# Attention laid out in a new order: score groups cut anew, every PSUM bank counted, small results in `av`'s spare columns

## The chip, the core and the metric

The kernel runs on one NeuronCore of a Trainium2 chip, as one program. The metric is the device time of one launch in microseconds. The profile is one execution of that program as the hardware profiler recorded it; times in it count from its first instruction.

## What is computed

Three layers follow one another: an attention with a memory term, a mixture of experts whose tokens are assigned greedily, and a dense layer with a maximum of three products. The change touches the first alone.

```python
def _attn_ref(q, k, v, M_prev, z_prev, beta):      # B, H, S, D = 4, 8, 576, 64
    scores = scale * np.matmul(q, k.transpose(0, 1, 3, 2))
    scores = np.where(causal, -1000000000.0, scores)
    scores = scores - scores.max(-1, keepdims=True)
    a = np.exp(scores)
    a /= a.sum(-1, keepdims=True) + 1e-09
    local = np.matmul(a, v)
    ...
    mem_out = mem_ret / mem_norm                   # phi(q) @ M_prev, phi(q) @ z_prev
    g = 1.0 / (1.0 + np.exp(-beta))[None, :, None, None]
    return (g * mem_out + (1 - g) * local).astype(np.float32)

x = attn_out.transpose(0, 2, 1, 3).reshape(B * S, H * D)
x = _moe_ref(x, ...)      # 8 experts of 288 tokens each, chosen by descending logit
return _moe2_ref(x, ...)  # max(x @ w1, x @ w2, x @ w3) @ w_out
```

## The kernel before

Attention works on 16 pairs of heads. The two heads of a pair lie on partitions 0 to 63 and 64 to 127, so that two products with 64 rows each, one for each head, run beside one another on TensorE. The 576 queries and keys are five tiles `j` and `kb` of 128 (the last one 64).

For one pair the work is as follows.

- SP loads `KR`, `QN`, `MZ`, `V` and `VT`. ScalarE casts keys and queries to `KH` and `QH` (fp32r), VectorE takes the rests `KL` and `QL`.
- A first, coarse pass of scores finds each query's maximum. It comes in pieces (`piece`, L409): query tile 3 (keys up to 512), tile 2 (384), tiles 1 and 0 (256 and 128), and tile 4 through the spread operand `qj` (L406). Every piece writes two buffers of the ring `st`, five PSUM banks in all. VectorE masks and reduces them into `nm` (L418, L422), ten reductions a pair.
- The nine columns of maxima are cast (L451, `nmr`), transposed on TensorE (L455, which writes one more buffer of `st`), copied out (L459, `nmt`) and sent by three DMAs (L464, L466) into a row tile, also called `nm`, that the exact scores subtract.
- The exact scores come transposed (keys on partitions) in three groups (`score`, L582), each of which writes two buffers of `st`, one for each head. A key tile's columns are four products for each head: `KH` by `QH`, `KL` by `QH`, `KH` by `QL`, and the subtraction of `nm`. Group 0 is key tile 0 with queries 0 to 512; group 1 is key tile 0 with the last 64 queries and key tile 1 with its 448; group 2 is key tile 2 with 320 and key tile 3 with 192, and then key tile 4 (64 by 64) in two further buffers. ScalarE takes exp of each buffer into `pt` (L608, L606), GpSimd masks the diagonal (L629). With each group goes one piece of the coarse pass of the pair two further on.
- `av` (L622) multiplies `pt` by `V`: ten products for each head with 128 columns of weights and five with 64 (query tile 4). It gathers in `AV`, a tile of two banks, one for each head, of which 365 of 512 columns are used. VectorE normalises it (L655 to L670).
- Beside this: `mem` (L529, five products of `phi` and `MZ` in two parts), and a gate product (L481, five of `VT` and `wb`, whose last has 64 columns of weights), all into the bank `MEM`. The dense layer's weights are converted meanwhile (`conv`, L825 to L866).

Ahead of the first exact scores TensorE runs 78 small products on zeros (L746, `warm`), spread between what it waits for.

The order of all this is made when the program is built. Each piece of work is a task with a key (10 for each pair, plus a number of the table `PRIO`), a cost for each engine that may run it, its predecessors, and the buffers that it takes. `Plan.run` schedules them greedily: of the tasks that could start earliest by the costs and by a table of latencies it takes the one with the smallest key. A task that takes a buffer of a full ring waits for the users of the oldest one. The engines then run their instructions strictly in the order so found. In `Plan.run` the count for a task that takes several buffers of one ring reads

```python
for b in t.new:
    k = len(b.ring.made) - b.ring.n
    if k >= 0:
        users += b.ring.made[k].users
```

and `made` grows only when the task is placed, so that each of the task's buffers looks at the same, oldest one.

## Time and profile before

| | us |
|---|---|
| time, median of 3 runs | 861.74 (859.13 to 865.17) |
| time of the profiled execution | 861.3 |
| its span, first to last instruction | 859.6 |
| TensorE busy in the span | 818.2 (95%) |
| VectorE busy | 552.6 (64%) |
| ScalarE busy | 341.5 (40%) |
| TensorE's granted clock, 0 to 20 us and 20 to 40 us | 1.00 and 0.66 |
| first exact scores start | 25.36 |
| second pair's exact scores start | 41.31 |
| last pair's exact scores start | 257.60 |

Attention takes the first 271 us; from there to about 300 us the first expert's tokens are chosen, mostly on VectorE, and the rest is the experts and the dense layer. `PE` is TensorE's matmuls, `PEld` its weight loads, `SPq` the DMA issues on SyncE's queue. A "busy" TensorE is one with a matmul in flight.

### The profile page before, as it was taken

To read this page: it belongs to the slowest core of one execution; us is meant where nothing else is said; L and a number is where in the kernel's file an instruction comes from. 1 tells how busy PE (TensorE), PEld (TensorE's weight loads), DVE (VectorE), ACT (ScalarE), POOL (GpSimd) and SP (SyncE) were. 2 spreads that over 40 slices of the span, in tenths; PEclk is the share of its full clock that TensorE was granted. 3 is DMA by queue.
4 is the path that set the end of the run, shared out by engine and by line. 5 is a ranking of instruction groups with operands and counts; after the bars stand their busy time and mean duration, and the time that the engine had idled before them with its cause. 6 is when DMAs were issued, how large, how long until landed. Compare 5 with 4: busy or idle time off the path is not lost.

```text
span 859.6 us, 17881 instructions
## 1 busy us (share of the span) xinstructions
PE 818.2 (95%) x6906; PEld 756.0 (88%) x6906; DVE 552.6 (64%) x1610; ACT 341.5 (40%) x871; POOL 102.2 (12%) x241
## 2 busy tenths in 40 slices
PE   8899999999996599999999999999999999999996
PEld 6788888888785499999999999999999999999996
DVE  7578889878834787886864874873774643532321
ACT  2567666566545432234214214313412422522311
POOL 2212112113212100101010010002002011000001
PEclk9699999999998599999999999999999999999999
DMA  5544655645402541425104404402412541450000
GB/s 157 164 142 142 194 159 176 192 145 168 148 5 70 134 105 37 135 91 175 50 29 146 76 18 127 106 1 94 121 48 60 165 42 36 151 46 26 26 1 38
DMA packets 39606, 84.80 MB, mean 99 GB/s; under 512 B 11552, under 2 KB 14304, under 8 KB 39520
## 3 DMA queue, kind: packets, MB, share of 16 engines
q1 hardware_dynamic: 35648, 72.87, 30.1%
q0 software_dynamic: 3872, 10.78, 4.3%
q8 instruction: 54, 0.88, 0.5%
q14 instruction: 32, 0.26, 0.1%
HBM read 72.77 MB, written 9.74 MB: 96 GB/s over the span
## 4 chain that ended last, share of the span: by engine, by line
PE 74%; issue 16%; DVE 5%; ACT 3%; POOL 1%; DMA 0%; DVEq 0%; POOLq 0%; ACTq 0%
PE av L622 12%; PE w L1300 10%; PE w L1302 10%; PE w L1301 10%; PE st L582 6%; PE acc L1300 5%; PE acc L1301 5%; PE acc L1302 5%; PE mem L529 3%; PE mem L481 2%; PE rps L1042 2%; ACT x L552 1%; PE st L409 1%; PE av L746 1%; DVE junk L422 1%
## 5 line engine op out<-in xcount | busy, mean ns | idle before, releaser
L1300 PE MATMUL w<-yh,mh 128*128 128x288 f32 x576 | 174.1, 302 | 0.0
L1302 PE MATMUL w<-yh,ml 128*128 128x288 f32 x576 | 169.8, 295 | 0.0
L1301 PE MATMUL w<-yl,mh 128*128 128x288 f32 x576 | 169.5, 294 | 0.0
L622 PE MATMUL av<-V,pt 128*128 128x112 f32 (+1 forms) x960 | 112.5, 266 | 0.3 <-DVE r L689 0.3
L1300 PEld LDWEIGHTS w<-yh,mh 128*128 128x128 f32 x576 | 108.6, 189 | 2.7
L1301 PEld LDWEIGHTS w<-yl,mh 128*128 128x128 f32 x576 | 108.3, 188 | 2.9
L622 PEld LDWEIGHTS av<-V,pt 128*128 128x128 f32 (+1 forms) x960 | 98.6, 173 | 13.7 <-issue 8.9
L1302 PEld LDWEIGHTS w<-yh,ml 128*128 128x128 f32 x576 | 108.3, 188 | 0.0
L1270 DVE TENSOR_TENSOR wlo<-wraw,whi 128x1024 fp32r<-128x1024 f32 x64 | 78.2, 1222 | 36.0 <-ACT whi L1266 35.8
L1407 DVE TENSOR_TENSOR mt<-w,mt 128x288 f32<-128x288 f32 x96 | 43.6, 454 | 80.2 <-PE w L1302 79.3
L422 DVE CUSTOM_DVE_ANT_0 junk<-st,mask 128x384 bf16<-128x384 f32 (+3 forms) x144 | 66.2, 460 | 27.2 <-PE st L409 14.7
L1266 ACT CAST whi<-wraw 128x1024 fp32r<-128x1024 f32 x64 | 66.8, 1049 | 30.7 <-PE acc L1301 21.5
L1301 PE MATMUL acc<-hl,whi 128*128 128x288 f32 x256 | 76.0, 297 | 1.4 <-DVE hl L1218 0.9
L1300 PE MATMUL w<-xhi,whi 128*128 128x288 f32 x256 | 76.5, 299 | 0.0
L1302 PE MATMUL w<-xhi,wlo 128*128 128x288 f32 x256 | 76.3, 298 | 0.2 <-DVE wlo L1270 0.2
L1300 PE MATMUL acc<-hh,whi 128*128 128x288 f32 x256 | 76.3, 298 | 0.0
L1301 PE MATMUL w<-xlo,whi 128*128 128x288 f32 x256 | 76.2, 298 | 0.0
L1302 PE MATMUL acc<-hh,wlo 128*128 128x288 f32 x256 | 75.3, 294 | 0.0
L1162 ACT CAST gc<-mt 128x32 fp32r<-128x32 f32 (+2 forms) x72 | 17.5, 243 | 140.8 <-DVE mt L1407 140.8
L608 ACT ACTIVATE pt<-st 128x512 f32<-128x512 f32 x96 | 52.8, 610 | 39.3 <-PE st L582 39.3
L1218 DVE SCALAR_TENSOR_TENSOR hl<-w,hh 128x288 fp32r<-128x288 f32 x64 | 29.2, 456 | 60.7 <-ACT hh L1212 60.6
L1243 POOL DMA_INDIRECT xg<-xd,tidx x24 | 24.1, 1002 | 351.2 <-PE w L1302 240.1
(236 smaller groups left out, 1727.3 us busy)
## 6 DMA issues: line engine op xcount, KB each, us to landing
wraw<-in_wr SPq DMA_DIRECT2D x64, 512.0 KB
m2raw<-in_m2w SPq DMA_DIRECT2D x12, 512.0 KB
V<-in_v SPq DMA_DIRECT2D x16, 365.0 KB
KR<-in_kN SPq DMA_DIRECT2D x16, 288.0 KB
QN<-in_qN SPq DMA_DIRECT2D x16, 288.0 KB
VT<-in_vT SPq DMA_DIRECT2D x16, 288.0 KB
xd<-x SPq DMA_DIRECT2D x16, 256.0 KB
m2raw<-in_m2w SPq DMA_DIRECT2D x12, 256.0 KB
```

Source lines behind the costliest of these rows:

```text
L422: V.tensor_tensor_reduce(out=junk[:, :w], in0=o.s[x][:, c:c + w], in1=m, scale=1.0, scalar=-3.0e38, op0=OP.add, op1=OP.max, accum_out=r.nm ...
L529: PE.matmul(MEM[:m, 2 * C * jj:2 * C * jj + 2 * C], r.phi[:, 128 * j:128 * j + m], r.MZ, start=True, stop=True)
L582: PE.matmul(d[:kr, c:c + z - a], neg[q, :kr] if wt is None else wt[q, k], mv[q, a:z], start=x == 0, stop=x == 3)
L608: A.activation(r.PT[:, i, 512 * gi:512 * gi + 512], o.t[i], AF.Exp, scale=0.125)
L622: PE.matmul(AV[:m, i, j * C:j * C + w], r.PT[:, i, o:o + m], r.V[:, c:c + w], start=kb == 0, stop=kb == j)
L1218: V.scalar_tensor_tensor(lo(), src(), 0.0, hi().bitcast(F32), op0=OP.max, op1=OP.subtract)
L1266: A.copy(x.W[fb][0], x.RAW[fb])
L1270: V.tensor_sub(x.W[fb][1], x.RAW[fb], x.W[fb][0].bitcast(F32))
L1300: nc.tensor.matmul(o, wh, rh, start=start, stop=False)
L1301: nc.tensor.matmul(o, wh, rl, start=False, stop=False)
L1302: nc.tensor.matmul(o, wl, rh, start=False, stop=stop)
L1407: V.tensor_max(q.mt, o.pt[:, :T], q.mt)
```

## The change

- The score groups are cut anew: group 0 is key tile 0 with queries 0 to 256 and key tile 1 with 128 to 384; group 1 key tile 0 with 256 to 576 and key tile 3; group 2 key tile 2 with 256 to 576 and key tile 1 with 384 to 576 (and, as before, key tile 4). The layout of `pt` follows (`COLS`).
- `Plan.run` counts each buffer that a task takes of a ring for itself. It also knows a price for a change between products with 64 and with 128 rows (`SWITCH`), and keeps TensorE off a bank of `AV` whose readers are not done (`held`).
- Of the coarse pass of query tile 4 the last 64 columns, and the transposed maxima, no longer take buffers of `st`: they go into columns 384 to 512 of `AV`.
- The last products of `mem` and of the gate get all 128 columns of weights: `phi` and `VT` become fixed tiles of 640 columns with zeros at the end.
- The first pairs' `KR` and `QN` are loaded first; the first pair's maxima become urgent work (`CRIT`); costs of DMA issues and all of `PRIO` have new numbers.

After attention the instructions of every engine stand in the same order as before.

```diff
+COLS = {(0, 0): 0, (0, 1): 128, (0, 2): 512, (0, 3): 640, (0, 4): 768, (1, 1): 256, (1, 2): 384, (1, 3): 1344, (1, 4): 1472,
+        (2, 2): 1024, (2, 3): 1152, (2, 4): 1280, (3, 3): 832, (3, 4): 960, (4, 4): 1536}
...
-        "T": (-1.2, 4.7, 5.8), "qj": "POOL", "nslack": 600, "A": (4.1, 6.4, 7.6, 8.7, 8.8), "norm": 15.3, "gate": 6, "m2": (4, 6.0, 10),
+        "phi": -3.6, "mem": (-0.3, 4.8), "memx": "ACT", "T": (-0.8, 4.2, 1.2), "qj": "POOL", "nslack": 600,
+        "A": (3.8, 6.6, 6.1, 9.4, 11.9), "norm": 13.6, "gate": 6, "m2": (4, 6.0, 7.8), "tmg": (1.1, 4.1, 12.7, 10.2), "lag": 6}
...
+WAIT, LD = 200, 700
+SWITCH = 135
...
-                blocked, users = False, []
+                users, taken = [], {}
                 for b in t.new:
-                    k = len(b.ring.made) - b.ring.n
-                    if k >= 0:
+                    k = len(b.ring.made) + taken.get(b.ring, 0) - b.ring.n
+                    taken[b.ring] = taken.get(b.ring, 0) + 1
+                    if 0 <= k < len(b.ring.made):
                         users += b.ring.made[k].users
+                users += held.get(t.bank, [])
...
-                    if e == "PE" and now < self.cold:
-                        c *= 2
+                    if e == "PE":
+                        c = c * (1 + (now < self.cold)) + SWITCH * (t.mode != mode)
...
+PHI = cs.tile([128, 640], F32, name="phi")
+    VT = [cs.tile([128, 640], F32, name=f"vt{k}") for k in range(BUFS["VT"])]
...
+        k1 = (-27, -26, -13.85)[p] if p < 3 else k0
...
-        tK = load("KR", [128, S], kN[b, pp], k0 - 3 * (p == 0), 1200)
+        tK = load("KR", [128, S], kN[b, pp], k1, LD)
...
-            o.bs, o.deps, o.key = [Buf(R["st"]) for _ in range(2)], [tqh, tkh, tj], key
+            tail = cuts[0][0] == 4
+            o.bs, o.deps, o.key = [Buf(R["st"]), Buf(R["aq" if tail else "st"])], [tqh, tkh, tj], key
...
+                    o.s = [ps.tile([128, 512], F32, name="st", bufs=BUFS["st"]) for _ in o.bs[tail:]] + [AV[:, 1, 384:]] * tail
...
-        kn = n + W["N"]
-        bn = Buf(R["st"])
+        kn = n + W["N"] if p else CRIT - 10
+        bn = Buf(R["an"])
...
-            r.pn = ps.tile([128, 512], F32, name="st", bufs=BUFS["st"])
-            PE.matmul(r.pn[:9, :128], r.nmr, identr, start=True, stop=True)
+            PE.matmul(AV[:9, 0, 384:], r.nmr, identr, start=True, stop=True)
...
-                PE.matmul(MEM[:rows(j), 4 * C + 16 * j:4 * C + 16 * j + w], r.VT[:, 128 * j:128 * j + rows(j)],
+                PE.matmul(MEM[:, 4 * C + 16 * j:4 * C + 16 * j + w], r.VT[:, 128 * j:128 * j + 128],
...
-                    m = rows(j)
-                    PE.matmul(MEM[:m, 2 * C * jj:2 * C * jj + 2 * C], r.phi[:, 128 * j:128 * j + m], r.MZ, start=True, stop=True)
+                    PE.matmul(MEM[:, 2 * C * jj:2 * C * jj + 2 * C], r.phi[:, 128 * j:128 * j + 128], r.MZ, start=True, stop=True)
...
-        groups = [[(0, 0, 512)], [(0, 512, 576), (1, 128, 576)], [(2, 256, 576), (3, 384, 576)]]
+        groups = [[(0, 0, 256), (1, 128, 384)], [(0, 256, 576), (3, 384, 576)], [(2, 256, 576), (1, 384, 576)]]
```

The first place is TensorE in the middle of a pair, from the end of one score group to the start of the next (`QL,KH` and `nm,neg` are the third and fourth products of a group; L409, and L429 after, is the coarse pass). Before, groups 1 and 2 stand back to back:

```order
L582 MATMUL st<-QL,KH 128x448 x2
L582 MATMUL st<-nm_129,neg 128x448 x2
L409 MATMUL st<-KH,QH 128x384 x2
L582 MATMUL st<-QH,KH 128x320 x2
L582 MATMUL st<-QH,KL 128x320 x2
```

and after, where group 2 comes first:

```order
L606 MATMUL st<-QL,KH 64x64 x2
L606 MATMUL st<-nm_129,neg 64x64 x2
L429 MATMUL st<-KH,QH 128x256 x2
L429 MATMUL st<-KH,QH 128x128 x2
L647 MATMUL av<-V,pt_131 64x73 x10
L506 MATMUL mem<-wb,vt_138 128x112 x4
L506 MATMUL mem<-wb,vt_138 128x16
L606 MATMUL st<-QH,KH 128x320 x2
```

The ten `av` products of query tile 4 and the gate's five moved between the two groups; the group that follows is the last of the pair.

The second place is TensorE where the first pair's exact scores begin. Before, both of the first products for the gate's constants (`wb,m2raw`), the second pair's transposed maxima and the first part of `mem` stand ahead of them:

```order
L746 MATMUL av<-warm 128x256
L765 MATMUL mem<-wb,m2raw 64x8 x8
L455 MATMUL st<-identr,nmr 9x128
L765 MATMUL mem<-wb,m2raw 64x8 x8
L529 MATMUL mem<-MZ,phi 128x146 x3
L582 MATMUL st<-QH,KH 128x512 x2
```

After, one set of `wb,m2raw` and then group 0 (eight rows, of which the last two stand here) come first:

```order
L606 MATMUL st<-QL,KH 128x256 x2
L606 MATMUL st<-nm_128,neg 128x256 x2
L429 MATMUL st<-KH,QH 128x512 x2
L553 MATMUL mem<-MZ,phi 128x146 x3
L479 MATMUL av<-identr,nmr 9x128
L426 MATMUL st<-KH,qj_126 128x512
L426 MATMUL av<-KH,qj_126 128x64
```

`mem`, the second set of `wb,m2raw` and the second pair's maxima moved behind the first score group, and the maxima and the last 64 coarse columns now write `av`.

The third place is SP's queue at the start, before:

```order
L349 DMA KR<-in_kN 128x576
L349 DMA QN<-in_qN 128x576
L349 DMA MZ<-in_mz 128x146
L349 DMA VT<-in_vT 128x576
L349 DMA V<-in_v 128x730
L275 DMA wb<-in_wg 64x4x8 x6
```

and after:

```order
L363 DMA KR<-in_kN 128x576
L363 DMA QN<-in_qN 128x576
L363 DMA KR<-in_kN 128x576
L363 DMA QN<-in_qN 128x576
L363 DMA MZ<-in_mz 128x146
L363 DMA V<-in_v 128x730
L373 DMA vt_137<-in_vT 128x576
L283 DMA wb<-in_wg 64x4x8 x6
```

The second pair's `KR` and `QN`, which stood behind the six `wb` transfers, now stand ahead of them; the third pair's follow right behind `wb`, and the first pair's maxima (`nm`) come before the second pair's `MZ`, `V` and `VT`.

## Rows read from the trace of the kernel before

**Rows 1.** Busy time by stretch: us, then busy us and instructions of each engine, PEclk, DMA

```profile
56.99:242.01 185.02, 176.71 (x1668) 152.29 (x1668) 154.45 (x484) 118.06 (x335) 39.10 (x129) 1.00 0.53 161
25.36:41.31 15.95, 15.21 (x113) 12.91 (x112) 8.30 (x30) 9.31 (x26) 3.59 (x10) 0.64 0.38 125
```

**Rows 2.** Waits, whole span: engine, what waited, releaser: us, times, longest

```profile
PE st L582 <- ACT pt L608: 7.4, 12, 1.1
```

**Rows 3.** Timeline of TensorE, one pair: start, us, line, out<-in, shape [idle before]

```profile
61.90 0.30 PE L582 MATMUL st<-QH,KH 64*128 64x64 f32 x2
...
63.25 0.34 PE L409 MATMUL st<-KH,QH 64*128 64x384 f32 x2
63.43 0.30 PE L582 MATMUL st<-QH,KH 64*128 64x320 f32 x1
64.64 0.41 PE L582 MATMUL st<-QH,KH 64*128 64x320 f32 x1 [0.91 <-ACT pt L608]
...
65.19 0.24 PE L582 MATMUL st<-QH,KH 64*128 64x192 f32 x1
```

**Rows 4.** Timeline of TensorE, group 2 of a late pair

```profile
248.34 0.31 PE L582 MATMUL st<-QH,KH 64*128 64x320 f32 x2
...
248.93 0.25 PE L582 MATMUL st<-QH,KH 64*128 64x192 f32 x2
...
249.36 0.20 PE L582 MATMUL st<-QH,KH 64*64 64x64 f32 x2
```

**Rows 5.** Timeline of TensorE from `av` into group 0

```profile
54.58 2.48 PE L622 MATMUL av<-V,pt 128*128 128x112 f32 x20
56.99 0.50 PE L582 MATMUL st<-QH,KH 64*128 64x512 f32 x2
...
58.03 0.39 PE L409 MATMUL st<-KH,QH 64*128 64x512 f32 x2
```

**Rows 6.** The same stretch asked from 56.72 on, so four of the twenty

```profile
56.45 0.61 PE L622 MATMUL av<-V,pt 128*128 128x112 f32 x4
```

**Rows 7.** Timeline of all engines at the start

```profile
6.14 0.75 DVE L501 SCALAR_TENSOR_TENSOR phi<-QN,ph 128x576 f32<-128x576 f32 x1
...
7.41 0.69 DVE L422 CUSTOM_DVE_ANT_0 junk<-st,mask 128x512 bf16<-128x512 f32 x1 [0.52 <-PE st L409]
...
10.36 1.26 PE L481 MATMUL mem<-wb,VT 128*128 128x112 f32 x10
...
11.56 2.36 PE L746 MATMUL av<-warm 128*128 128x256 bf16 x20
...
12.70 0.21 DVE L422 CUSTOM_DVE_ANT_0 junk<-st,mask 128x64 bf16<-128x64 f32 x1
...
16.95 0.30 PE L455 MATMUL st<-identr,nmr 128*9 128x128 f32 x1
...
18.29 1.24 SPq L466 DMA_DIRECT2D nm<-nmt  x2
...
19.44 0.64 PE L765 MATMUL mem<-wb,m2raw 128*64 128x8 f32 x16
...
22.59 0.67 ACT L295 CAST KH<-KR 128x576 fp32r<-128x576 f32 x1 [1.59 <-DMA KR<-in_kN]
...
23.63 1.80 PE L529 MATMUL mem<-MZ,phi 128*128 128x146 f32 x6 [2.24 <-issue]
...
25.36 0.79 PE L582 MATMUL st<-QH,KH 64*128 64x512 f32 x2
```

**Rows 8.** Waits of VectorE between 56.99 and 242.01 us, the two longest

```profile
DVE junk L422 <- PE st L409: 7.5, 18, 0.9
DVE rm L533 <- PE mem L529: 7.1, 14, 1.2
```

**Rows 9.** Timeline of a pair: coarse pass of query tile 4, and its second reduction

```profile
68.07 0.51 PE L406 MATMUL st<-KH,qj 128*128 128x512 f32 x2
...
70.84 0.21 DVE L422 CUSTOM_DVE_ANT_0 junk<-st,mask 128x64 bf16<-128x64 f32 x1
```

More of the change, by code (lines that the diff above doesn't have):

```diff
@@ L115, in __init__ @@
         self.new, self.use, self.end, self.lat, self.slack = [], [], None, None, 0
-        self.left, self.nexts = 0, []
+        self.left, self.nexts, self.mode, self.bank, self.readers = 0, [], 0, None, []
 class Plan:
@@ L148, in run @@
     def run(self):
-        free, order, now = {}, [], 0
+        free, order, now, mode, held = {}, [], 0, 0, {}
         for t in self.tasks:
@@ L198, in run @@
             t.end, t.eng = end, e
+            if e == "PE":
+                mode = t.mode
+                if t.readers:
+                    held[t.bank] = held.get(t.bank, []) + t.readers
             now = max(now, best[0])
@@ L275, in ldw @@
                 nc.sync.dma_start(WB[64 * i:64 * i + 64, a, :, i], wg.rearrange("(c i d) e -> i d c e", i=2, d=64)[i])
-    twb = add(-14.8, {"SP": 1200}, ldw)
+    twb = add(-13.9, {"SP": 4000}, ldw)
     cdone = constants(g, tc, consts, beta, add)
     R = {n: Ring(k) for n, k in BUFS.items()}
-    R["av"], R["mem"], R["xl"] = Ring(1), Ring(1), Ring(1)
+    for x in ("av", "mem", "an", "aq", "xl"):
+        R[x] = Ring(1)
     def tile(name, shape, dt=F32):
@@ L401, in fS @@
                 if not hasattr(o, "s"):
-                    o.s = [ps.tile([128, 512], F32, name="st", bufs=BUFS["st"]) for _ in o.bs]
+                    o.s = [ps.tile([128, 512], F32, name="st", bufs=BUFS["st"]) for _ in o.bs[tail:]] + [AV[:, 1, 384:]] * tail
                 for j, c in cuts:
@@ L430, in alone @@
         def alone(o):
-            o.after(add(o.key, {"PE": o.cost + 130}, o.fn, o.deps, new=o.bs + o.first, use=o.use))
+            t = add(o.key, {"PE": o.cost}, o.fn, o.deps, new=o.bs + o.first, use=o.use)
+            t.mode = 64 * (o is not r.last)
+            k = len(tred)
+            o.after(t)
+            if o is r.last:
+                t.bank, t.readers = 1, tred[k + 1:]
         ks = n + W["S"]
@@ L436, in pair @@
                               [(i, c, w, 4 * i + j) for i in range(2) for j, c, w in ((1, 0, 256), (0, 256, 128))]))
+        r.last = piece(ks + W["last"], [(4, 0)], [(0, 0, 512, 8), (1, 0, 64, 9)])
         if p < AHEAD:
@@ L439, in pair @@
                 alone(o)
-        r.last = piece(ks + W["ds"] * 3, [(4, 0)], [(0, 0, 512, 8), (1, 0, 64, 9)])
         alone(r.last)
         yield r
-        kn = n + W["N"]
-        bn = Buf(R["st"])
+        kn = n + W["N"] if p else CRIT - 10
+        bn = Buf(R["an"])
         def fx(e):
@@ L469, in pair @@
         t = add(kn, {"ACT": 100}, fn0, [t], new=[bf["nmr"]], use=[bf["nm"]])
-        t.slack = W["nslack"]
-        t = add(kn, {"PE": 110}, fn1, [t], new=[bn], use=[bf["nmr"]])
-        t = add(kn, {"ACT": 140}, fn2, [t], new=[bf["nmt"]], use=[bn])
-        r.tN = add(kn + .1, {"SP": 1500}, fn3, [t, tnm[p] if p < len(NM) else None], new=[bf["NM"]], use=[bf["nmt"]], lat=NLAT)
+        t.slack = W["nslack"] if p else 0
+        tt = add(kn, {"PE": 110}, fn1, [t], new=[bn], use=[bf["nmr"]])
+        t = add(kn, {"ACT": 140}, fn2, [tt], new=[bf["nmt"]], use=[bn])
+        tt.bank, tt.readers = 0, [t]
+        r.tN = add(kn + .1, {"SP": 1900}, fn3, [t, tnm[p] if p < len(NM) else None], new=[bf["NM"]], use=[bf["nmt"]], lat=NLAT)
         bG = Buf(R["mem"])
@@ L492, in phi1 @@
         def phi1(e):
-            r.phi = tile("phi", [128, S])
+            r.phi = PHI
             r.ph = tile("ph", [128, S])
@@ L596, in score @@
             b2 = (s.bs if s else [Buf(R["st"]) for _ in range(2)]) if gi == 2 else s.bs if s else []
-            cost = 4 * sum(mm(z - a) for kb, a, z in gr) + 280 * (gi == 2) + 130 + (s.cost if s else 0)
+            cost = 4 * sum(mm(z - a) for kb, a, z in gr) + 280 * (gi == 2) + (s.cost if s else 0)
             t = add(key, {"PE": cost}, fT, [tkh, tqh, tkl, tql, r.tN] + (s.deps if s else []), new=bt + b2 + (s.first if s else []),
                     use=[bf[x] for x in ("KH", "QH", "KL", "QL", "NM")] + (s.use if s else []))
+            t.mode = 64
             for x in [gi] + [3] * (gi == 2):
@@ L639, in pair @@
             for i in range(2):
-                need = [mk[x] for x in range(j + 1)] + ([ex[x, 1] for x in range(2)] if j == 4 else [])
-                outs.append(add(n + W["A"][j] + .5 * i, {"PE": (225, 450, 675, 900, 330)[j]}, fAV(i, j),
+                need = [mk[x] for x in range(j + 1)] + [ex[x, 1] for x in range(2)] * (j > 1)
+                outs.append(add(n + W["A"][j] + .5 * i, {"PE": (225, 450, 675, 900, 650)[j]}, fAV(i, j),
                                 need + outs[-2:][:1] * (j > 0) + [r.tV] + (fill if p == 0 else []), new=[bf["av"]] if not outs else [],
                                 use=[bf["PT"], bf["V"]] + ([bf["av"]] if outs else [])))
+                outs[-1].bank = i
         h = 2 * pp
```

44 lines of the change are left out of this document (24 added, 20 removed).

## The prediction, made before the changed kernel ran

> **What bounds the kernel now.** I read the busy time by stretch first. From the second pair's region to the last but one (56.99 to 242.01 us, twelve pairs) TensorE has a matmul in flight for 176.71 of 185.02 us, VectorE works 154.45, ScalarE 118.06 [rows 1]. So a pair takes 185.02/12 = 15.42 us, and 14.73 of them are TensorE's work; VectorE's 12.87 come second. The reader should see both: TensorE sets the end, and VectorE is close behind it. The waits then say what TensorE's idle time is: the exact scores wait for ScalarE's exp 12 times, 7.4 us in all [rows 2]. The timeline shows the place. Group 2 starts one product at 63.43, and the product for the other head starts at 64.64, after an idle 0.91 us that ends with exp [rows 3]. Groups 1 and 2 stand back to back, and the second of group 2's two banks is one that exp has not left yet. That is what the old count in the planner would do: it asks for the users of one bank where the task takes two or more. Third, the start. The first exact scores come at 25.36 us, and until 41.31 the clock granted to TensorE averages 0.64 of 2.4 GHz; ahead of that stretch TensorE had idled for 2.24 us, up to `mem` at 23.63 [rows 1, 7].
>
> The sum is made against the profiled execution, 861.3 us with a span of 859.6; the median of the three runs is 0.4 higher. Behind attention no engine's order changes, so what TensorE's last `av` product gains, the whole gains.
>
> **The stall in group 2.** Counted right, the buffers of a group are free when it starts, and now ten `av` products and the gate stand between two groups. What goes is the idle time and a restart behind it. From the first product of group 2 to its first 192-wide one it takes 65.19 - 63.43 = 1.76 us in the stalled pair [rows 3] and 248.93 - 248.34 = 0.59 in one without a stall [rows 4]. Of the 1.17 between them 0.91 is idle and 0.26 is two heads that no longer run abreast. Twelve stalls: 7.4 + 12 x 0.26 = **10.5 us** off. The lower bound is 7.4 less whatever the next wait takes, which I count below.
>
> **Other pieces.** The old group 1 (64 and 448 columns) takes 63.25 - 61.90 = 1.35 us [rows 3]. The new one that replaces it has the widths of group 2 (320 and 192), which takes 249.36 - 248.34 = 1.02 [rows 4]. That is 0.33 for each of 16 pairs, **5.3 us** off. Group 0 has two pieces of 256 where one of 512 stood. A 512-wide group takes 58.03 - 56.99 = 1.04 us [rows 5]. A 256-wide step of both heads should cost between a 192-wide one, 0.43/4 = 0.107, and a 320-wide one, 0.59/4 = 0.148 [rows 4]; eight are 0.86 to 1.18. The middle is 1.02, so I take no change; the bounds are 2.9 us better and 2.2 worse over 16 pairs.
>
> **Changes of the shape of a product.** Twenty `av` products start from 54.58 on, and the last four of them at 56.45, so sixteen take 1.87 us, 0.117 each. The four and the step into 64-row products take 56.99 - 56.45 = 0.54 [rows 5, 6], which is 0.07 more than four of 0.117. I take 0.07 for each change of rows or of weight columns. From the first exact scores on, the order of before has 204 such changes and that of after 158: there is one more group in and out, but the ends of `mem` and gate no longer change to 64 columns and `av`'s ten products of tile 4 are no longer split. 46 x 0.07 = **3.2 us** off. If only a change of rows costs, it is a loss: 67 become 95, 28 x 0.07 = 2.0 us more. These are the bounds. The rows priced here step from 128 rows to 64 at unchanged columns; that a step in columns costs the same is my choice, and the other reading is a rival below.
>
> The Trainium skill speaks against the extra group: TensorEngine Tiling (Array Packing), section Key Properties, says that a change of the tiling mode drains TensorE. The 0.07 us of these rows agree that there is a price. By that rule for any change of tile size the sum is the one below; for rows alone it is 5.2 us longer.
>
> **The start.** Three things move. VectorE's first ten reductions run from 7.41 to 12.91 us, 5.5 us [rows 7]. Before them stood `phi` (0.75 us at 6.14), which now comes later, and fewer `warm` products stand ahead of the scores; so they can start at about 6.5 and end at 12.0. The first pair's maxima are transposed at 16.95 now [rows 7], long after they are there, since TensorE's order puts the second pair's scores and the gate ahead. After the change they come right behind the reductions, about 12.5. That is 4.4 us earlier, and so are the three DMAs, the last issued by 15.1 instead of 19.53 (18.29 + 1.24). Their landing is bounded by 25.36, 5.8 us after issue; so at the worst 20.9, and the subtraction is only the fourth product of a group. TensorE itself still has a last coarse piece (0.51 [rows 9]), the gate (1.26), a coarse piece of 0.4, 26 `warm` products (20 take 2.36, so 3.07) and one set of small products for `m2raw` (0.64) [rows 7]: 12.5 + 0.3 + 5.9 = 18.7. I take 18.7 for the first exact scores, **6.7 us** earlier; the bounds are 20.9 and, if the reductions lose all of `phi`'s 0.75 and half a us of waiting besides, 17.5. The second pair's keys come from a transfer that no longer stands behind the six `wb`; ScalarE's cast of the third pair's at 22.59, which waited for its DMA and held up the copy that `mem` waited for [rows 7], has its data early too.
>
> **The clock.** From 25.36 to 41.31 the mean is 0.64, so (1 - 0.64)/0.5 = 72% of 15.95 us, 11.5 us, ran at 1.2 GHz; TensorE was busy 15.21/15.95 of it [rows 1]. Without the idle time at 21.4 to 23.6 I expect the full clock, and half of 11.5 x 0.95 comes back: **5.5 us** off. If the fall comes anyway this is 0.
>
> **What is given back.** Work that stood ahead of the first scores now stands behind them: `mem`'s three products, 25.36 - 23.63 = 1.73 us at half the clock [rows 7], 0.9 at the full one; five `warm` products 0.6; one set of `m2raw` 0.6; and a wait for the scaled `MZ`, which needs ScalarE's copy behind the second pair's maxima, about 0.5. **2.6 us** on.
>
> **The next wait.** TensorE's work in a pair becomes 14.73 less 0.24 (restart), 0.33 and 0.20, or 13.96 us. VectorE's is between 154.45/12 = 12.87 and (185.02 - 14.6)/12 = 14.2, where 14.6 us are its two longest waits and whatever else it idles is counted as work [rows 1, 8]. So it is 92% to over 100% full. The casts, loads and exps have room (ScalarE 118.06/12 = 9.84). I take a period of 14.2, a new wait of 0.25 us in each of 14 pairs, **3.5 us** on; the bounds are 0 and 1.0 a pair (14 us).
>
> Sum: 10.5 + 5.3 + 3.2 + 6.7 + 5.5 - 2.6 - 3.5 = 25.1 us. 861.3 - 25.1 = **836.2 us**.
>
> **Rivals.**
>
> *VectorE becomes the bound.* The planner's costs put a 512-wide masked reduction at 680 ns with its own formula; the ten reductions in a row take 5.5 us in the trace [rows 7] where the formula sums to 4.6. An order planned with too fast a VectorE, and 92% or more full, runs late on every pair. For it: the row of VectorE; against it: the same formula made the order of before, where VectorE itself waited. At the upper bound, 14 us instead of 3.5, the time is 847.
>
> *The clock falls again.* `mem` still waits for ScalarE and GpSimd behind the first group, and TensorE's idle time there could again be followed by half the clock. Against it: the wait is about 0.5 us, not 2.24. The time is 842.
>
> *Only a change of rows costs.* Then the extra group is a loss of 2.0 instead of a gain of 3.2. For it: the price above was read from rows alone; against it: nothing in the rows. The time is 841.
>
> *Nothing at the stall.* The wait for exp comes back at another bank of the ring, since there are still five and a group takes four. Then the 10.5 do not come, and the extra group in and out buys nothing (5.2): 852, at the edge of no change. Against it: a pair takes 13 buffers of the ring instead of 15.
>
> *Slower: the shared bank.* The coarse pass of tile 4 now writes 64 columns of the second head's `AV` bank, and `av` products of that head wait until VectorE has read them. VectorE's read starts 70.84 - 68.07 = 2.8 us after that piece starts [rows 9]. In the new order group 0 (1.04), a coarse piece (0.3), four `av` products (0.9) and three of `mem` (0.85) stand between, with the piece itself 3.6 us. Each us beyond that by which VectorE is late holds `av`, and with it every pair. To lose all 25.1 us in 15 pairs it must come 1.7 later, at 5.3 us; that is the point from which the kernel is slower, and at 6.0 us it takes 872. The Trainium skill bears on this: PSUM — Partial Sum Buffer, section PSUM bank collisions raise a hardware error, says that two engines must not touch one bank at once even at different columns, so the wait cannot be left out. No run so far shows such a collision.
>
> **Chances and range.** The forecast with its own bounds (827 to 843) has 0.52, VectorE as the bound 0.17, the clock 0.10, rows alone 0.10, nothing at the stall 0.07, the shared bank 0.04. The range that leaves out 2 in 10 is 827 to 849: its lower end has the better bounds of pieces, start and next wait together (2.9 + 1.2 + 3.5) and a little more for a dearer step, its upper end VectorE's bound with a few us of the others. A measurement of this kernel can tell about 1% from no change, 8.6 us. Faster by more than that (under 853) are the first four cases but for the far end of the second, and half of nothing at the stall, 0.88; within 1% is 0.08, slower 0.04.
>
> **What would show it.** Right: no row in which group 2 or 1 idles on exp; the first exact scores at 18 to 19 us and the second pair's near 31; clock 1.00 from 20 to 40 us; 14.0 to 14.4 us between the first scores of neighbouring pairs; the last `av` product near 245 instead of 271. Wrong: a period over 14.8, with `av` or the coarse pass waiting for VectorE (the second case); a granted clock of 0.5 between 20 and 40 us; or `av` behind `mem` idle for VectorE's read of `av` (the last case).

## The result, and the profile after

| | before | after |
|---|---|---|
| time, median, us | 860.43 (858.72 to 865.17, 4 runs) | 836.68 (836.02 to 836.83, 4 runs) |
| ratio | | 0.9714 (95%: 0.9673 to 0.9755) |
| span of the profiled execution | 859.6 | 834.3 |
| first exact scores start | 25.36 | 20.05 |
| second pair's | 41.31 | 32.00 |
| third pair's to 14th pair's, a pair | 15.45 | 14.63 |
| TensorE's last `av` product ends | 270.98 | 248.57 |
| from there to the end of the span | 588.6 | 585.7 |

The forecast was 836.2. The sum comes out; its terms do not all, and the runs below say which. Of the signs that the prediction named, two came (no row in which the scores wait for exp, the full clock from 20 to 40 us) and four just missed: the first scores at 20.05 us instead of 18 to 19, the second pair's at 32.0 instead of 31, a pair in 14.63 instead of 14.0 to 14.4, the last `av` product near 248.6 instead of 245.

Busy time of after by stretch (us, then busy us and instructions of TensorE, its weight loads, VectorE, ScalarE and GpSimd, TensorE's granted clock, DMA share, GB/s): the first two pairs and the eleven steady ones.

```profile
20.08:45.53 25.45, 25.04 (x305) 22.96 (x303) 18.86 (x63) 18.13 (x57) 6.70 (x17) 1.00 0.58 187
45.53:206.49 160.96, 152.10 (x1630) 139.99 (x1629) 148.13 (x460) 109.51 (x312) 43.84 (x123) 1.00 0.57 182
```

The same two stretches of before, cut at the same events; they answer to [rows 1].

```profile
25.36:56.99 31.63, 30.52 (x266) 26.16 (x265) 20.06 (x68) 18.98 (x55) 5.83 (x16) 0.82 0.41 126
56.99:226.98 169.99, 162.17 (x1531) 139.82 (x1531) 143.84 (x451) 110.25 (x311) 36.31 (x123) 1.00 0.55 167
```

In the steady pairs TensorE's work fell from 162.17/11 = 14.74 to 152.10/11 = 13.83 us a pair. Its idle time did not fall: 7.82/11 = 0.71 before, 8.86/11 = 0.81 after. What changed is who is waited for. Waits of TensorE in after, from 45.53 to 206.49 us (who waited, for whom: us, times, longest):

```profile
PE av L647 <- DVE tmp L688: 3.4, 7, 0.5
PE mem L506 <- ACT x L576: 3.1, 7, 0.7
PE av L647 <- issue: 1.4, 3, 0.6
PE av L647 <- DVE nm L442: 0.6, 1, 0.6
PE mem L553 <- DVE phi L526: 0.2, 1, 0.2
```

The row of the exact scores that wait for exp [rows 2] is gone. In its place `av` waits for VectorE's normalisation of the pair before, and the gate waits for ScalarE's `x`, which itself waits for VectorE's `g`. The timeline of one pair, of TensorE and VectorE, shows the first kind:

```profile
127.81 0.42 DVE L442 CUSTOM_DVE_ANT_0 junk<-st,mask 128x256 bf16<-128x256 f32 x1
...
128.53 0.29 DVE L442 CUSTOM_DVE_ANT_0 junk<-st,mask 128x128 bf16<-128x128 f32 x1 [0.28 <-ACT pt L631]
...
128.74 0.17 DVE L681 SCALAR_TENSOR_TENSOR r<-av,c 128x10 f32<-128x10 f32 x1
...
129.19 0.91 DVE L688 TENSOR_TENSOR tmp<-av,r 128x720 f32<-128x720 f32 x1
...
130.25 0.67 PE L647 MATMUL av<-V,pt 128*128 128x112 f32 x4 [0.54 <-DVE tmp L688]
```

The last `av` products of the pair before ran from 125.20 for 1.48 us, so they had ended at 126.68. VectorE comes to their normalisation (`r`, its reciprocal, `tmp`) two us later, behind four reductions, and the next `av` has to wait for it. The three waits that the view calls `issue` end in the same way, 0.10 us after `tmp`; so 4.8 of the 8.9 us are waits for the normalisation.

The start of after answers to [rows 7]:

```profile
7.13 0.69 DVE L442 CUSTOM_DVE_ANT_0 junk<-st,mask 128x512 bf16<-128x512 f32 x1 [0.92 <-POOL qj L304]
...
12.71 0.60 PE L774 MATMUL av<-warm 128*128 128x256 bf16 x4 [0.86 <-DVE nm L442]
...
13.60 0.23 PE L479 MATMUL av<-identr,nmr 128*9 128x128 f32 x1
...
18.73 0.82 PE L774 MATMUL av<-warm 128*128 128x256 bf16 x6 [0.82 <-DVE nm L442]
...
19.48 0.64 PE L793 MATMUL mem<-wb,m2raw 128*64 128x8 f32 x16
20.05 0.39 PE L606 MATMUL st<-QH,KH 64*128 64x256 f32 x2
...
21.42 1.01 PE L553 MATMUL mem<-MZ,phi 128*128 128x146 f32 x6
```

The clock of the first 20 to 40 us, of before and of after:

```profile
20.00:40.00 20.00, 16.57 (x127) 13.81 (x123) 8.73 (x34) 10.85 (x32) 4.23 (x12) 0.66 0.51 168
```

```profile
20.00:40.00 20.00, 19.59 (x248) 17.85 (x247) 14.44 (x53) 13.98 (x46) 6.29 (x16) 1.00 0.54 177
```

### The profile page after: what moved, and what is told of

It reads as the page before. It is cut to its first block, busy times and chain, and to the rows that moved or that the text cites. A ratio compares the mean times of both kernels' runs of the same rounds, so it can differ in the third digit from the quotient of the medians.

```text
span 834.3 us, 18159 instructions
## 1 busy us (share of the span) xinstructions
PE 795.2 (95%) x7034; PEld 748.6 (90%) x7034; DVE 554.3 (66%) x1610; ACT 340.2 (41%) x871; POOL 109.9 (13%) x244
## 4 chain that ended last, share of the span: by engine, by line
PE 66%; issue 17%; DVE 12%; ACT 2%; DMA 1%; POOL 1%; SPq 0%; DVEq 0%; POOLq 0%; ACTq 0%
PE w L1328 10%; PE w L1330 10%; PE w L1329 10%; PE av L647 8%; PE acc L1328 5%; PE acc L1329 5%; PE acc L1330 5%; PE st L606 4%; DVE junk L442 4%; PE rps L1070 2%; PE mem L553 1%; DVE m2b L870 1%; PE mem L506 1%; DMA QN<-in_qN 1%; PE rps L1141 1%
## 5 line engine op out<-in xcount | busy, mean ns | idle before, releaser
L647 PE MATMUL av<-V,pt 128*128 128x112 f32 (+1 forms) x960 | 108.1, 262 | 6.5 <-DVE tmp L688 3.4
L1190 ACT CAST gc<-mt 128x32 fp32r<-128x32 f32 (+2 forms) x72 | 17.5, 243 | 141.1 <-DVE mt L1435 141.1
L442 DVE CUSTOM_DVE_ANT_0 junk<-st,mask 128x512 bf16<-128x512 f32 (+3 forms) x128 | 62.5, 488 | 16.0 <-PE st L429 4.6
```

Source lines behind the costliest of these rows:

```text
L442: V.tensor_tensor_reduce(out=junk[:, :w], in0=o.s[x][:, c:c + w], in1=m, scale=1.0, scalar=-3.0e38, op0=OP.add, op1=OP.max, accum_out=r.nm ...
L647: PE.matmul(AV[:m, i, j * C:j * C + w], r.PT[:, i, o:o + m], r.V[:, c:c + w], start=kb == 0, stop=kb == j)
```

## The experiments

The theory is that of the prediction, with its size of the next wait corrected: the stall was real, and VectorE now sets TensorE's idle time. The rivals ask whether the stall was worth anything, whether VectorE is late because it is full or because of what stands where, and whether start, pieces and shapes are worth their terms. Where the text gives the end of attention, it is the end of the last `av` product in the profiled execution (270.98 before, 248.57 after).

**The count alone**, in the kernel before:

```diff
-                    k = len(b.ring.made) - b.ring.n
-                    if k >= 0:
+                    k = len(b.ring.made) + taken.get(b.ring, 0) - b.ring.n
+                    taken[b.ring] = taken.get(b.ring, 0) + 1
+                    if 0 <= k < len(b.ring.made):
```

> The kernel before with one edit: the planner counts every bank that a task takes. Keys, pieces, loads and costs stay, so av products now stand between groups 1 and 2 in most pairs. If the stall in group 2 is worth what the prediction says (7.4 us idle and 0.26 us of restart twelve times), the row of exact scores waiting for pt is gone and the period of the pairs falls from 15.4 to 14.7-15.0 us: 850 us (847 to 854). If the wait only comes back at another bank or another engine, the period stays near 15.4 and the time at 858 to 862.

870.89 us (865.92 to 873.21), ratio to before 1.0139 (1.0112 to 1.0167): slower than before, which neither theory had. The wait for exp is gone from the view of waits. From the second to the 14th pair, twelve pairs:

```profile
PE mem L530 <- ACT x L553: 3.2, 4, 2.0
PE av L623 <- issue: 2.4, 1, 2.4
PE av L623 <- POOL MZ L296: 1.9, 2, 1.5
```

```profile
35.17:231.78 196.61, 184.60 (x1687) 159.55 (x1685) 159.45 (x493) 121.84 (x346) 42.73 (x131) 0.96 0.52 160
```

A pair takes 16.4 us. The `av` and `mem` products that now stand between the groups need VectorE's normalisation, its `g` and GpSimd's masks earlier than the old keys and costs provide them. In the longest wait, 2.44 us up to 93.12, the view names nothing, but the normalisation before it ends at 93.02:

```profile
92.12 0.90 DVE L663 TENSOR_TENSOR tmp<-av,r 128x720 f32<-128x720 f32 x1
```

The two waits that the view puts down to GpSimd's copy of `MZ` end 0.10 us after `tmp` as well. The granted clock falls to half four times within attention, 20.5 us in all, at 22.2, 93.8, 128.0 and 162.1 us, each time within 2.4 us after TensorE had idled for 1.2 to 2.4 us. So the count is needed for the new order, but is worth nothing by itself: the old keys with the right count are worse than with the wrong one.

**The stall put back**, with the order otherwise that of after. The first try used the old count and a key for group 1 right behind that of group 2 (`"T": (-0.8, 1.3, 1.2)`), which also moved other work.

> The kernel after with the old count of banks, and with the key of group 1 set right behind that of group 2, so that these two groups stand back to back again in about every second pair or more (as groups 1 and 2 did in before). Pieces, start and costs are those of after. If the stall is what the old order cost, exact scores wait for exp again, 0.6 us or more each time, and the time is 843 us (840 to 848). If VectorE is now the bound of a pair, TensorE's wait for exp hides in the time that it would wait for VectorE anyway: 835 to 839 us.

852.0 us (847.2 to 857.1, 9 runs); attention ends at 259.61. The groups stand together in about half of the pairs, and scores wait for exp again, but other waits came with the moved work:

```profile
PE st L606 <- ACT pt L633: 3.9, 6, 1.3
PE av L647 <- ACT nmt L483: 2.6, 2, 2.0
PE mem L553 <- ACT V L304: 2.2, 4, 1.1
```

It is slower than the stall theory said, and not a clean test of it. The second try moves nothing else on TensorE: behind the planner, group 1 with its coarse piece goes right behind group 2 in eleven pairs. (In three of them some of VectorE's conversion steps and its first step of the normalisation change places too.)

```diff
+    for p in range(2, 15):
+        i, k = (next((x for x, t in enumerate(order) if getattr(t, "group", None) == (p, g)), -1) for g in (2, 1))
+        if 0 <= i < k:
...
+            order[i + 1:k + 1] = [t for t in order[i + 1:k] if t not in gone] + [order[k]] + [t for t in order[i + 1:k] if t in gone]
```

> The kernel after with one move in each of the pairs whose two groups lie apart: group 1 with its coarse piece is put right behind group 2, ahead of the ten or fourteen av products and the gate that stood between them. Nothing else is moved on any engine, and no pieces, shapes or buffers change. If the stall of two neighbouring groups is worth what the prediction says, exact scores wait for exp in each of these pairs again, 0.6 us or more, and restart. VectorE's lateness hides some of it, at most the 0.7 us that TensorE waits for VectorE in a pair now: 843 us (839 to 848). If TensorE's place in the pair is set by VectorE whatever stands where, the waits change their names and the time is 835 to 838 us.

877.95 us (872.13 to 880.7), 41 us slower than after and far above what either theory allowed; attention ends at 288.40. Waits and busy time over the eleven steady pairs:

```profile
PE st L616 <- ACT pt L643: 21.8, 11, 2.2
PE av L657 <- DVE tmp L698: 0.8, 3, 0.3
```

```profile
45.45:244.41 198.96, 174.92 (x1629) 160.38 (x1627) 150.14 (x460) 109.38 (x312) 39.77 (x123) 0.88 0.49 147
```

A pair takes 18.1 us instead of 14.6: 1.4 more idle (24.04/11 = 2.19 against 0.81) and 2.1 more in products (15.90 against 13.83), because the clock falls behind each of the eleven waits and the mean is 0.88. VectorE's rows have nearly gone from the waits, as they should if TensorE is late itself. One stall, on ScalarE and TensorE:

```profile
70.31 1.34 ACT L586 ACTIVATE x<-mem,rm 128x64 f32<-128x64 f32 x6 [1.92 <-DVE g L576]
71.50 1.12 ACT L643 ACTIVATE pt<-st 128x512 f32<-128x512 f32 x2
```

```profile
69.61 0.36 PE L616 MATMUL st<-QH,KH 64*128 64x320 f32 x1
72.19 0.46 PE L616 MATMUL st<-QH,KH 64*128 64x320 f32 x1 [2.21 <-ACT pt L643]
```

It is more than twice the stall of before [rows 3], since exp stands behind the six scalings of `x` in ScalarE's queue, and these wait for VectorE. So neighbouring groups do stall, and what a stall costs depends on its length above all by the clock: behind the twelve of before, at most 1.1 us long, the clock stayed full, behind these eleven of 1.6 to 2.25 it fell each time. The Trainium skill, TensorE: Matmul & The Clock Gate, section HAM oscillation — how this bites in real kernels, tells of a loop in which a DMA wait of about 3 to 5 us in every turn sends the clock down again; these eleven pairs agree that it can happen in every turn, with 0.88 as the mean, but here 1.6 to 2.25 us were enough.

**Pieces.** After with the score pieces of before:

```diff
-        groups = [[(0, 0, 256), (1, 128, 384)], [(0, 256, 576), (3, 384, 576)], [(2, 256, 576), (1, 384, 576)]]
+        groups = [[(0, 0, 512)], [(0, 512, 576), (1, 128, 576)], [(2, 256, 576), (3, 384, 576)]]
```

(the places in `pt`, what `av` waits for, and the keys of groups 1 and 2 go with them, so TensorE's order changes too).

> The kernel after with the score pieces of before (512; 64 and 448; 320 and 192, with the 64-row piece in the last), the right count, the new start and the new loads. The prediction takes 0.33 us a pair for the 64-wide piece: 842 us (840 to 845), with TensorE busy 14.2 us in a pair instead of 13.8. If the pace of a pair is VectorE's, the pieces cost nothing: 836 to 838 us, with TensorE busier and its idle time shorter by the same amount.

845.0 us (843.9 to 846.1), at the upper edge of the forecast. Attention ends 4.2 us later than in after (252.80). The work is there as forecast, 155.55/11 = 14.14 us a pair against 13.83:

```profile
46.80:210.47 163.67, 155.55 (x1541) 138.70 (x1541) 145.93 (x459) 112.49 (x320) 38.25 (x124) 1.00 0.57 178
```

That is 0.31 a pair where the prediction had 0.33. The other 5.8 us of the difference in span lie behind attention, where the order is the same; see below.

**Shapes.** After with 64 columns of weights again in the last product of `mem` and of the gate:

```diff
-                PE.matmul(MEM[:, 4 * C + 16 * j:4 * C + 16 * j + w], r.VT[:, 128 * j:128 * j + 128],
+                PE.matmul(MEM[:rows(j), 4 * C + 16 * j:4 * C + 16 * j + w], r.VT[:, 128 * j:128 * j + rows(j)],
```

(and `mem` in the same way).

> The kernel after with the last product of mem and of the gate cut to 64 weight columns again, as in before; the order is the same on every engine. TensorE then changes its columns three more times in a pair (into and out of the last product of mem, into that of the gate). If each change costs the 0.07 us of the prediction, TensorE has 0.2 us more work in a pair: 837.5 to 840.5 us, the less the more of it hides in its waits for VectorE. If only a change of rows costs, 835.5 to 837.2 us and no more work in the rows of these lines.

844.03 us (842.0 to 846.5), above both ranges. Attention ends at 253.08, 4.5 us later, for 48 more changes of columns: 0.09 each; the rest lies behind attention.

```profile
46.41:209.75 163.34, 156.19 (x1629) 139.30 (x1627) 148.22 (x460) 109.67 (x313) 42.24 (x123) 1.00 0.57 180
```

TensorE has 156.19/11 - 13.83 = 0.37 us more in flight in a pair and idles 0.16 less, so the period is 14.85 instead of 14.63. A change of weight columns costs as much as the change of rows that the prediction had priced at 0.07, or a little more; the reading that only rows cost is out. Of the Trainium skill's rule in TensorEngine Tiling (Array Packing), section Key Properties, on the drain at a change of the tiling mode this is the price here: 0.09 to 0.12 us, for columns too.

**The start.** After with the first three pairs' loads and the first pair's maxima in their old places:

```diff
-        k1 = (-27, -26, -13.85)[p] if p < 3 else k0
+        k1 = k0 - 3 * (p == 0)
...
-        kn = n + W["N"] if p else CRIT - 10
+        kn = n + W["N"]
```

> The kernel after with the start of before: the first three pairs' loads at their old places and the first pair's maxima transposed in their old turn; from the fourth pair on TensorE's order is that of after. If the start is worth what it seemed (first exact scores 5.3 us earlier), and the clock falls again because TensorE idles ahead of mem, the first scores come near 25.4, the granted clock is near 0.5 for some 12 us behind them, and the time is 847 us (844 to 850). If only the position counts and the clock stays full (more warm products stand ahead of mem here than in before), 842 us (840 to 844). If VectorE sets the pace of the first pairs whatever the start, under 839 us.

840.68 us (840.0 to 843.6), 4.0 slower than after; attention ends 3.8 us later (252.35). But the first exact scores do not come at 25.4:

```profile
20.63 0.38 PE L606 MATMUL st<-QH,KH 64*128 64x256 f32 x2
...
25.50 0.91 PE L793 MATMUL mem<-wb,m2raw 128*64 128x8 f32 x16 [1.70 <-ACT x L576]
```

They are 0.6 us later than in after. What is lost comes behind them: TensorE idles 1.70 us in the middle of the first pair, and 6.8 us at half the clock follow (25.7 to 32.5). So the early loads and maxima are worth some 4 us, and not by an earlier first score: it is the second pair's scores that come at 37.3 instead of 32.0. What is left to have moved the first scores forward is that `mem`, a set of `m2raw` products and the second pair's maxima no longer stand ahead of them; no run shows this alone, and with the count alone in before they came at 22.92.

**The clock at the start.** Before, with 20 `warm` products in the 2.24 us for which TensorE idles ahead of the first `mem` [rows 7]:

```diff
+                for q in range(20 * (p == 0 and part == 0)):
+                    PE.matmul(AV[:, 1, :256], warm[:, :128], warm[:, :256], start=True, stop=True)
```

> The kernel before with 20 products of warm put ahead of the first pair's first mem, into the 2.24 us for which TensorE idles there; everything else is as before. If that idle time is what the clock falls after, the granted clock stays at 1.00 behind it and 11.5 us at half the clock become some 6 shorter: 854 us (852 to 857), with the second pair's first scores near 35.5 instead of 41.3. If the clock falls for another reason (it falls in the same place in spite of the products), 859 to 862 us.

860.45 us (856.7 to 862.7, 10 runs), ratio 0.9995 (0.9971 to 1.002): no gain. In its profiled execution the first pair runs at 0.87 instead of 0.64,

```profile
24.08:37.61 13.53, 11.96 (x113) 10.26 (x112) 8.37 (x32) 9.16 (x26) 3.06 (x9) 0.87 0.48 156
```

the time at half the clock at the start falls from 13.7 us to 3.4, and attention ends 3.8 us earlier (267.22). Over ten runs none of it is left in the median. The profiled execution of before had a mean clock of 0.972; 17 runs of before beside this one had a median of 0.977, this kernel 0.979. So idle time and a fall belong together in these traces, but the term of 5.5 us was read from one execution, whose clock was lower than in most. What the fall costs in a usual one isn't settled.

**VectorE lighter.** After, with one of VectorE's three conversion steps of the dense weights on 64 of 512 columns; the rest of that step is left out.

```diff
-            V.scalar_tensor_tensor(u.t1, u.t0.bitcast(I32), 3, u.t1, op0=OP.logical_shift_left, op1=OP.bitwise_or)
+            V.scalar_tensor_tensor(u.t1[:, :64], u.t0.bitcast(I32)[:, :64], 3, u.t1[:, :64], op0=OP.logical_shift_left, op1=OP.bitwise_or)
```

> The kernel after with one of the three VectorE steps that make the dense weights (the shift by 3 with the or) done on 64 of 512 columns; the rest of these columns keeps its old value, so part of the dense weights is left out. The order is the same on every engine, and VectorE has some 0.5 us less to do 24 times, about 0.8 us less in a pair. If the 0.8 us for which TensorE idles in a pair are VectorE being late, TensorE's idle time shrinks to 0.3 or less, the period falls from 14.63 to 14.0-14.2 and the time is 830 us (827 to 833). If they come from the order itself or from ScalarE, 834.5 to 837 us.

829.95 us (829.0 to 833.6), 6.7 less than after. TensorE's waits over the eleven pairs, and the busy time:

```profile
PE av L647 <- DVE nm L442: 0.5, 1, 0.5
PE av L647 <- issue: 0.3, 1, 0.3
PE mem L553 <- DVE phi L526: 0.2, 1, 0.2
```

```profile
45.40:198.46 153.06, 151.39 (x1628) 140.04 (x1628) 137.65 (x458) 109.77 (x313) 40.34 (x123) 1.00 0.61 192
```

The period is 13.91, TensorE's work 13.76, its idle time 0.15. That VectorE sets TensorE's idle time in after is shown. The rows of `x` are gone with those of `tmp`: ScalarE's part in them was VectorE's.

**Less work on VectorE by moving it.** Two tries to have this gain and leave nothing out. First, the subtractions for the low part of the dense weights on GpSimd (`V.tensor_sub` to `G.tensor_sub` at L894):

> The kernel after with the 24 subtractions that make the low part of the dense weights (512 columns each) on GpSimd instead of VectorE, at the same places in the order. If VectorE's lateness is the wait and GpSimd has room (it is busy 27% of a pair), TensorE idles some 0.5 us less in a pair: 831 us (828 to 834). If GpSimd becomes late in turn, so that the masks of pt or the scaled MZ stand behind a subtraction, the waits of av and mem on GpSimd grow and the time is 837 to 845 us.

838.55 us (835.6 to 840.1). The text above counts 24 of them, but the line runs eight times, all in the first four steady pairs; two of the steady pairs take 14.0 us, the others 14.4 to 14.8 as before, and attention ends 2.1 us earlier (246.47). TensorE waits for GpSimd in none of them. Second, the addition of `tmp` to `x` (L692), once in every pair, on GpSimd:

> The kernel after with the addition of the normalised av to x (640 columns, 0.82 us once a pair) on GpSimd instead of VectorE, at the same places in the order. It lies in every pair, where the 24 subtractions of the other attempt lay in few, and nobody on TensorE waits for it. If VectorE's lateness is what TensorE waits for, this takes 0.8 us a pair from VectorE as the lighter shift did: period 14.0-14.2, 831 us (828 to 834). If GpSimd's last mask of a pair, which stands behind the addition in its queue, comes too late for av, or the shared work slows VectorE, 835 to 840 us.

839.31 us (837.7 to 841.2), attention ends at 249.33: nothing gained, though 0.82 us left VectorE in each pair. Two reasons stand in the rows. VectorE's `g` addition beside it, which reads two tiles in SBUF, became longer in four of the eleven pairs. The mean in after, and two of the eleven here:

```profile
L696 DVE TENSOR_TENSOR g<-g,tmp 128x80 f32<-128x80 f32 x11 | 2.6, 239 | 0.2
```

```profile
57.18 1.59 DVE L696 TENSOR_TENSOR g<-g,tmp 128x80 f32<-128x80 f32 x1
...
130.79 0.24 DVE L696 TENSOR_TENSOR g<-g,tmp 128x80 f32<-128x80 f32 x1
```

The first began while GpSimd's addition ran (from 57.02, for 1.65 us) and took 1.59 us; the second began just ahead of it (130.84) and took no longer than in after. The reductions of 384 columns, which read PSUM, took 554 ns (553 in after). The Trainium skill, GPSIMD Engine Reference, section 1. Specifications, says that the two engines share their interfaces to SBUF and collide where VectorE has two inputs there; the first row agrees, the second shows no loss. And the work taken away stood behind `tmp`, where TensorE no longer waits: `av` waits for `tmp` 4.1 us here against 3.4. The last six steady pairs, where no `g` is longer, show this second reason alone, after and here:

```profile
119.36:206.46 87.10, 81.96 (x885) 75.65 (x883) 78.29 (x244) 57.56 (x168) 24.18 (x83) 1.00 0.55 172
```

```profile
120.00:207.16 87.16, 81.63 (x886) 75.32 (x884) 75.42 (x237) 57.80 (x169) 33.25 (x89) 1.00 0.53 169
```

VectorE has 0.48 us less to do in a pair, and the pair takes as long, 14.53 us against 14.52.

**The place instead of the load.** After with the normalisation (`r`, its reciprocal, `tmp`) ahead of those of the four reductions that stand between the pair's last `av` product and it; no work changes.

```diff
+            red = [x for x in range(k + 1, n) if getattr(order[x], "red", 0) in (128, 256)]
+            if red:
+                rest = [t for t in order if t not in norm]
+                i = rest.index(order[red[0]])
+                order = rest[:i] + norm + rest[i:]
```

> The kernel after with one move on VectorE in thirteen pairs: the three steps of the normalisation (r, its reciprocal, tmp) go ahead of those of the four reductions (256 and 128 columns) that stand between the pair's last av product and them, one to four of them, 0.4 to 1.5 us. No work is added or taken away, and TensorE's and ScalarE's orders stay. If TensorE waits for VectorE because of what stands ahead of these steps, not because VectorE is full, the rows of av waiting for tmp (3.4 us) and for nothing shown (1.4 us) go and the time is 832.5 us (830 to 834.5), and what stays is mem waiting for x. If VectorE's load sets the period, the wait only moves to the reductions' readers and the time stays at 835.5 to 838 us.

838.92 us (834.9 to 840.5), above both ranges, but attention ends at 245.81, 2.8 us earlier. In the same six pairs, where after took 14.52 us each, the period is 83.94/6 = 13.99, and only `mem`'s waits are left:

```profile
PE mem L517 <- ACT x L587: 1.2, 5, 0.4
PE mem L564 <- DVE phi L537: 0.5, 1, 0.5
```

```profile
119.58:203.52 83.94, 82.20 (x884) 75.89 (x882) 76.56 (x242) 57.80 (x168) 23.15 (x83) 1.00 0.56 178
```

VectorE is busy 12.76 us a pair here, more than the 12.57 of the run before, in which TensorE waited for it. In two earlier pairs `av` waits, 1.5 and 0.9 us, for the reduction of the coarse columns in its own bank, which VectorE reaches late; ahead of the second the move had passed a conversion step and a `QL`. With the move in the eleven pairs without such a step:

> The kernel after with the normalisation moved ahead of the reductions as in the run before, but only in the eleven pairs in which nothing but reductions stands between, so that no rest QL and no conversion step of the dense weights is passed. In the run before attention ended 2.9 us earlier than in after although two pairs (the fourth and fifth of the steady ones) lost 0.8 us to a late reduction, and the whole was no faster, since the first expert's weights came late and the clock fell there. If that loss was a chance of where attention ends, attention now ends near 244.5 us, 4 us earlier than in after, and the time is 833 us (831 to 835). If each us gained in attention is given back behind it, 836 to 840 us.

835.19 us (834.6 to 839.6, 6 runs), between its two ranges, ratio to before 0.9685 (0.9661 to 0.9708); attention ends at 246.08. That is 1.5 us under after, and the intervals overlap. The loss of 0.9 us is gone, that of 1.5 us has stayed, so passing such a step was not its cause:

```profile
91.99 0.21 DVE L452 CUSTOM_DVE_ANT_0 junk<-av,mask 128x64 bf16<-128x64 f32 x1
...
92.26 0.70 PE L658 MATMUL av<-V,pt 128*128 128x112 f32 x4 [1.49 <-DVE nm L452]
```

So VectorE's lateness is in good part a matter of what stands ahead of three short steps, not of how full it is: the wait of `av` goes with VectorE's work unchanged.

**Behind attention** no order differs among after and its variants, and still the span from the last `av` product to the end was 585.7 us in after, 586.8 in the run on the start, 586.9 with VectorE lighter, 587.4 and 589.7 with work on GpSimd, 591.6 and 591.5 in the runs on pieces and shapes, 592.9 and 591.8 in the last two. In the run on shapes the first expert's weights are late:

```profile
306.33 1.04 ACT L1294 CAST whi<-wraw 128x1024 fp32r<-128x1024 f32 x1 [2.88 <-DMA wraw<-in_wr]
```

TensorE idles 1.55 us for the cast, and 6.8 us at half the clock follow; in after the same casts found their data. These transfers run while attention ends, so their landing may depend on when it does, but no run took this cause away by itself, and the spans do not follow the end of attention in order. Nor is one execution like another: that of the last run with the profile took 839.6 us as a whole, its other five 834.6 to 835.9. So how much of these differences belongs to a kernel, and how much to one execution, stays open.

## Why the prediction came out, point by point

- *The stall in group 2* (10.5 us): the wait for exp is gone, as forecast, and putting the groups together again brings it back. But its idle time is not gained: TensorE's idle time a pair went from 0.71 to 0.81. What remains of this term is the restart and the right to place other work between the groups.
- *The next wait* (0.25 us a pair): mis-sized. It is 0.8, and it is the one named, VectorE. The step that failed is "92% to over 100% full": VectorE is busy 92% in the steady pairs, and TensorE waits all the same, because the normalisation stands behind work that could wait. An average of busy time can't show this. The rival with VectorE as the bound was half right, for its reason but not its price: 14.63 us a pair, not over 14.8.
- *TensorE's work in a pair*: 13.96 forecast, 13.83 measured. Pieces 0.31 for 0.33; a change of columns 0.09 to 0.12 for 0.07, so the choice between rows and any change was right and a little low. Eight products of 256 columns were taken to cost as much as four of 512: eight steps took 20.05 to 21.09, 1.04 us, as one 512-wide group [rows 5]. Of the 0.91 us that TensorE's work lost in a pair, the pieces are 0.31 and three changes of columns 0.37; the 0.23 left is near the restart of 0.24, which no run took alone.
- *The start* (18.7, bounds 17.5 and 20.9): 20.05. The reductions start at 7.13 instead of 6.5, since the products through `qj` wait for GpSimd, and TensorE waits twice for VectorE (0.86 and 0.82). The reason given, early loads and maxima, was wrong for the first scores (0.6 us) and right for the first two pairs (3 us).
- *The clock at the start* (5.5): full in the profiled execution, as forecast, but filling the idle time alone gains nothing in the median. The size rests on one execution, and it is not confirmed.
- *Given back* (2.6, with half a us of waiting for `MZ`): `mem` starts at 21.42 right behind the coarse piece, no wait.
- *The shared bank*: `av` waits once for the reduction of the coarse columns in its bank (0.6 us), and the last ten `av` products wait 0.76 for VectorE to leave the bank. Nothing of the size of that rival, but its mechanism is there: the room was put at 3.6 us, and where the reduction started 4.26 us after its piece `av` waited 0.56, and 1.49 where it started at 5.19 (the last run).
- *"What TensorE's last `av` product gains, the whole gains"*: not in these two executions. 22.4 us were gained up to there and 2.9 behind it, and executions of one kernel differ by more than that (the last run, 834.6 to 839.6).

By stretch, forecast and measured: up to the first scores -6.7 and -5.3; the first two pairs -5.3 and -6.2; the eleven steady pairs -10.3 and -9.0; the rest of attention -2.8 and -1.9; behind it 0 and -2.9. The forecast terms of the pairs are split here evenly over 16 pairs, the new wait over the last 14. The misses, up to 2.9 us each, cancel to 0.2, so the closeness of the sum is chance, and the range was the better statement.

## What to carry over

When a stall is taken away, ask first which engine is late next, and at which instruction: here the idle time stayed as long as it was and only changed its name, and three short steps moved ahead of work that could wait shortened it where less work on that engine, at the wrong place, did not. A fix in a planner is worth only what its costs and keys make of it: the right count with the old numbers was 10 us slower than the wrong one. Of an idle TensorE, count the half clock that may follow as well as the wait: in the attention of these kernels it followed 19 of the 25 waits of 1.2 to 2.4 us, and no shorter one that stood by itself.

## What the runs showed of the hardware that was not expected

- Eleven waits of 1.6 to 2.25 us cost TensorE 1.4 us more idle time and 2.1 us more in its products in each pair, since the granted clock was at half for 3.4 or 6.8 us behind each of them (mean 0.88).
- A change of the columns of weights between two products costs about 0.1 us (48 of them 4.5 us), like a change of rows.
- A GpSimd addition of 640 columns takes 1.63 us. A VectorE addition of 80 columns that began while it ran took 0.78 to 1.60 us (four of eleven), one that began just ahead of it 0.24 (seven), as without it.
- The same instructions behind attention took 585.7 to 592.9 us in the profiled executions of after and its variants; why is open.
